# Attention by whole pairs of heads: 128-query tiles, plain float32 scores, single-bank ring, before two expert layers

## The chip, the cores and the metric

The kernel runs on one core of a Trainium2 chip. Five engines work from their own in-order queues: TensorE (PE, matrix products into PSUM), VectorE (DVE), ScalarE (ACT), GpSimd (POOL) and SyncE (SP, which here only issues transfers); they meet at semaphores. The metric is device microseconds of one execution, as a median of several.

## What is computed

```
# q, k, v: 2 batches x 12 heads x 448 positions x 64, float32
scores = q @ k.T / 8                    # causal: keys after the query are masked with -1e9
scores = scores - max(scores)
attn   = exp(scores);  attn = attn / (sum(attn) + 1e-9)
x      = attn @ v                       # to 896 tokens x 768
h      = x @ w_in;  g = max(h, 0) + alpha * min(h, 0);   x = g @ w_out      # 768 -> 2048 -> 768
h      = x @ w2_in; g = 0 if h <= -1, h if h >= 1, else (h + 1)**2 / 4;     out = g @ w2_out
```

The weights arrive as 64-bit floats.

## The kernel before

The 24 heads are taken as 12 pairs. A pair's q and k lie transposed in one tile (`qk_raw`): head 0 on partitions 0 to 63, head 1 on 64 to 127, so that the two heads of a score product occupy different halves of the rows of the PE array. The 448 queries of a head are four tiles of 112; tile i needs the first 112 (i + 1) keys. The loop at L451 walks over 48 tiles of 12 pairs. In step t it issues the scores of tile t, the exponentials and the normalisation of tile t - 1, the transposes of tile t - 3, the products with v of older tiles (first key chunk 7 steps behind, second 8, third and fourth 9), and the evacuation of a pair 10 steps behind. All of it is a hand-written order (`manual_schedule`): each engine executes its share in the order of the code.

For a tile with i > 0 the scores are three products of split operands (`qk_spl`: a rounded float32r part and the rest; L337 makes them, ACT the rounded part, POOL the rest); tile 0 uses the raw float32 values (L351). DVE reads the scores from PSUM, adds the mask and finds the row maximum in one operation (L363), ACT takes the exponential and its row sum (L373), DVE adds 1e-9 and inverts (L380, L381), POOL multiplies (L384), PE transposes 112 x 112 blocks (L394), ACT and DVE copy the result to `pt` (L400 to L405), and PE multiplies by v into `o_ps` (L413), both heads side by side in different column halves. The evacuation splits the result into x, a rounded part on ACT (L208) and the rest on DVE (L211).

On PE the groups of one pair come in this order: transposes of tile 2 (6), products with v of chunks 2 and 3 (224 and 112 columns of both heads), scores of tile 2 of the next pair (336 columns), transposes of tile 3 (8), scores of tile 3 (448), transposes of tile 0 (2), products with v of chunk 0 (448), scores of tile 0 (L351, 112), transposes of tile 1 (4), products with v of chunk 1 (336), scores of tile 1 (256). One plain float32 product is two instructions in the trace.

The 8 PSUM banks are three single ones for scores (`s_ps`), two tiles of two banks for transposes (`t_ps`) and one for `o_ps`. In the layers `new_banks` (L233) hands the same tiles out in turn, the two-bank tiles as two halves.

The weights come in chunks of 768 x 128 (first layer) through a ring of two raw buffers. A chunk is turned into a split pair by `magnitude` (L108, ACT), clamp (L124), low bits (L130), high bits (L136), last bits (L142, with a rounding copy on ACT, L145) and rest (L148), all on DVE but the two named. `prime` makes three chunks ready during the attention: from step 20 on it yields one operation in two of four steps. `early_tiles` issues products of the first layer for the x tiles that are ready, while the last pairs finish: 5 x 6 matmuls of the first output tile and 5 x 3 of the second. Then `run_layer` walks the four layers; its matmuls (L255) are 2304, with 448 columns each.

SP issues all loads in code order: per pair one transfer for q and k and one for v.

Of the kernel before, what the change touches and what calls it, by code (L numbers as in the profile page):

```python
# [22 lines left out]
def attention_moe_moe_kernel(ctx: ExitStack, tc: tile.TileContext, qk, v, w1, w2, w3, w4, alpha, out):  # L23
# [13 lines left out]
    W = [CP * (i + 1) for i in range(NQ)]  # L37
    OFF = [sum(W[:i]) for i in range(NQ)]
    TRI = sum(W)
# [6 lines left out]
    NSQ = 1  # L46
    NWARM = 9
# [10 lines left out]
    ident = const.tile([CP, CP], F32, tag="ident", name="ident")  # L58
    mask = const.tile([CP, S], F32, tag="mask", name="mask")
# [3 lines left out]
    def warm_up():  # L63

        z = const.tile([128, 512], F32R, tag="zero", name="zero")
        nc.vector.memset(f32(z), 0.0)
        for _ in range(NWARM):
            ps = ps_o.tile([128, 512], F32, tag="o", name="warm_ps")
            nc.tensor.matmul(ps, lhsT=z[:, :128], rhs=z, start=True, stop=True)  # L69

    def constants():
        nc.vector.memset(half, 0.5)
        make_identity(nc, ident)
        nc.gpsimd.memset(mask, 0.0)
        nc.gpsimd.affine_select(
            out=mask[:, S - CP:], in_=mask[:, S - CP:], compare_op=ALU.is_ge, fill=MASK,
            base=0, pattern=[[-1, CP]], channel_multiplier=1,
        )
# [154 lines left out]
    def new_banks():  # L233


        def one(pool, tag):
            return pool.tile([128, 512], F32, tag=tag, name="ps")

        while True:
            for singles in (((ps_s, "s"), (ps_s, "s")), ((ps_s, "s"), (ps_o, "o"))):  # L240
                for pool, tag in singles:
                    yield one(pool, tag)
                both = ps_t.tile([128, 1024], F32, tag="t", name="ps")
                yield both[:, :512]
                yield both[:, 512:]

    def new_tile():
        return next(banks)
# [58 lines left out]
    class Attention:  # L307
# [3 lines left out]

        PARTS = ((0, 0), (0, 1), (1, 0))

        def __init__(self, ap, ps_s, ps_t, ps_o):
            self.ap, self.ps_s, self.ps_t, self.ps_o = ap, ps_s, ps_t, ps_o
            self.raw, self.vraw, self.spl, self.pexp, self.st, self.pt, self.o = {}, {}, {}, {}, {}, {}, {}

        def load(self, p):
            t = self.raw[p] = self.ap.tile([2 * D, 2, S], F32, tag="qk_raw", name="qk_raw", bufs=3)
# [5 lines left out]
            t = self.vraw[p] = self.ap.tile([CP, NQ, 2, D], F32, tag="v_raw", name="v_raw", bufs=5)  # L328
            nc.sync.dma_start(out=t, in_=v[p])

        def split_qk(self, p, a, high=nc.scalar.copy, low=nc.gpsimd):
            t = self.raw[p]
            if a == 0:
                self.spl[p] = self.ap.tile([2 * D, 2, 2, S], F32R, tag="qk_spl", name="qk_spl", bufs=2)
            s = self.spl[p]
            n0 = NSQ * CP if a == 0 else 0
            high(s[:, a, 0, n0:], t[:, a, n0:])  # L337
            low.tensor_sub(s[:, a, 1, n0:], t[:, a, n0:], f32(s[:, a, 0, n0:]))

        def scores(self, p, i):  # L340
            if i == 0:
                self.pexp[p] = self.ap.tile([CP, 2, TRI], F32, tag="pexp", name="pexp", bufs=3)
                self.st[p] = self.ap.tile([CP, NQ, 3, 2], F32, tag="stat", name="stat", bufs=4)
            s, t = self.spl[p], self.raw[p]
            w = W[i]
            n = max(w, 256)
            ps = [self.ps_s.tile([128, 512], F32, tag="s", name="s_ps")[:CP] for _ in range(2)]
            if i < NSQ:
                for j in range(2):
                    r = slice(j * D, (j + 1) * D)  # L350
                    nc.tensor.matmul(  # L351
                        ps[j][:, :w], lhsT=t[r, 0, i * CP:(i + 1) * CP], rhs=t[r, 1, :w], start=True, stop=True
                    )
            for x, (a, b) in enumerate(self.PARTS if i >= NSQ else ()):
                for j in range(2):
                    r = slice(j * D, (j + 1) * D)
                    nc.tensor.matmul(  # L357
                        ps[j][:, :n], lhsT=s[r, 0, a, i * CP:(i + 1) * CP], rhs=s[r, 1, b, :n],
                        start=x == 0, stop=x == 2,
                    )  # L360

            for j in range(2):
                nc.vector.tensor_tensor_reduce(  # L363
                    out=self.pexp[p][:, j, OFF[i]:OFF[i] + w], in0=ps[j][:, :w], in1=mask[:, S - w:],
                    scale=-SCALE, scalar=3.0e38, op0=ALU.add, op1=ALU.min,
                    accum_out=self.st[p][:, i, 0, j:j + 1],
                )

        def expo(self, p, i):
            st = self.st[p]  # L370
            for j in range(2):
                e = self.pexp[p][:, j, OFF[i]:OFF[i] + W[i]]
                nc.scalar.activation(  # L373
                    out=e, in_=e, func=AF.Exp, bias=st[:, i, 0, j:j + 1], scale=-1.0,
                    accum_out=st[:, i, 1, j:j + 1],
                )

        def norm(self, p, i):
            st = self.st[p][:, i]
            nc.vector.tensor_scalar_add(st[:, 1], st[:, 1], 1e-9)  # L380
            nc.vector.reciprocal(st[:, 2], st[:, 1])  # L381
            for j in range(2):
                e = self.pexp[p][:, j, OFF[i]:OFF[i] + W[i]]
                nc.gpsimd.tensor_scalar(  # L384
                    out=e, in0=e, scalar1=st[:, 2, j:j + 1], scalar2=1.0, op0=ALU.mult, op1=ALU.mult
                )

        def transp(self, p, i):
            ps = self.ps_t.tile([128, 1024], F32, tag="t", name="t_ps")[:CP]
            ps = ps.rearrange("p (j n) -> p j n", j=2)[:, :, :S].rearrange("p j (c q) -> p j c q", q=CP)  # L390
            for j in range(2):
                for c in range(i + 1):
                    o = OFF[i] + c * CP
                    nc.tensor.transpose(ps[:, j, c, :], self.pexp[p][:, j, o:o + CP], ident)  # L394
            if i == 0:
                self.pt[p] = self.ap.tile([CP, 2, NQ, S], F32, tag="pt", name="pt", bufs=2)
            d = self.pt[p][:, :, :i + 1, i * CP:(i + 1) * CP]

            if i == 0:
                nc.scalar.copy(d, ps[:, :, :i + 1, :])  # L400
            elif i == 1:
                nc.vector.tensor_copy(d, ps[:, :, :i + 1, :])  # L402
            else:
                nc.scalar.copy(d[:, 0], ps[:, 0, :i + 1, :])
                nc.vector.tensor_copy(d[:, 1], ps[:, 1, :i + 1, :])  # L405

        def attnv(self, p, chunks):
            if 0 in chunks:
                self.o[p] = self.ps_o.tile([2 * D, 512], F32, tag="o", name="o_ps")
            ps, pt, vraw = self.o[p], self.pt[p], self.vraw[p]  # L410
            for c in chunks:
                for j in range(2):
                    nc.tensor.matmul(  # L413
                        ps[j * D:(j + 1) * D, c * CP:S], lhsT=vraw[:, c, j, :], rhs=pt[:, j, c, c * CP:S],
# [3 lines left out]
        def evac(self, p):  # L418
            b, m = divmod(p, NP // NB)
            interleave(evac_x(self.o.pop(p), m, b), [])  # L420

    with tc.manual_schedule():
        wts = Weights()
        ps_s, ps_t, ps_o = (
            ctx.enter_context(tc.tile_pool(name=f"ps_{n}", bufs=b, space=PSUM))
            for n, b in (("s", 3), ("t", 2), ("o", 1))
        )
        banks = new_banks()
        with ExitStack() as pa:
            ap = pa.enter_context(tc.tile_pool(name="attn", bufs=2))  # L430
            at = Attention(ap, ps_s, ps_t, ps_o)
            at.load(0)
            warm_up()
            nc.sync.dma_start(out=alpha_sb, in_=alpha)
            at.load(1)
            constants()
# [5 lines left out]
            NT = NP * NQ  # L442

            LE, LT = 1, 3
            LV = {7: (0,), 8: (1,), 9: (2, 3)}
            LX = 10
            PRIME = 20

            for t in range(NT + LX - 2):  # L451
                p, r = divmod(t, NQ)
                if t < NT:
                    at.scores(p, r)
                if t >= LX and (t - LX) % NQ == 0:
                    at.evac((t - LX) // NQ)
                if 0 <= t - LE < NT:
                    at.expo(*divmod(t - LE, NQ))
                    at.norm(*divmod(t - LE, NQ))
                if 0 <= t - LT < NT:  # L460
                    at.transp(*divmod(t - LT, NQ))
# [74 lines left out]
```

## Time and profile before

| | before |
|---|---|
| median of 3 runs | 586.44 us (584.26, 586.44, 595.68) |
| span of the profiled execution | 591.8 us |
| PE busy | 583.1 us (99%), 3009 matmuls |
| DVE busy | 442.3 us (75%) |
| ACT busy | 255.6 us (43%) |
| POOL busy | 161.6 us (27%) |
| matmuls of the layers (L255) | 240.2 + 238.6 us, 369 and 368 ns each, 2304 |
| granted TensorE clock, mean | 0.999 |

The shares of busy time are means over an attention part of some 120 us and four layers behind it. A busy PE is not PE at its peak, since matmuls are pipelined and an instruction's row also covers time in which it waits in the pipe; the distance from one start to the next tells more.

### The profile page before, as it was taken

How to read it: one execution, taken by the hardware profiler on the slowest of the kernel's cores; microseconds unless marked ns; L12 is line 12 of the kernel's file. 1: busy time of each engine (PE TensorE's matmuls, PEld its weight loads, DVE VectorE, ACT ScalarE, POOL GpSimd, SP SyncE). 2: the span in 40 equal slices, each digit the busy share in tenths (PEclk: the TensorE clock that was granted, in tenths of full speed). 3: DMA queues.
4: the chain of work that ended last, by engine and by line, in shares of the span. 5: the costliest groups of instructions: out<-in, count | busy, mean ns of one | idle time of the engine just before them, and what ended most of it. 6: DMA issues, size and time to landing. Idle time of an engine off the chain costs nothing.

```text
span 591.8 us, 8421 instructions
## 1 busy us (share of the span) xinstructions
PE 583.1 (99%) x3009; PEld 491.8 (83%) x3009; DVE 442.3 (75%) x894; ACT 255.6 (43%) x543; POOL 161.6 (27%) x190
## 2 busy tenths in 40 slices
PE   8999999999999999999999999999999999999997
PEld 3655555789999999999999999999999999999995
DVE  4899998488898898766657668888888867555740
ACT  3889888223333333333223325555555422222220
POOL 3777787223333343000000002333334300000000
PEclk9999999999999999999999999999999999999999
DMA  6533301113333222343324333333322244444420
GB/s 187 201 95 88 131 24 55 54 54 107 108 112 108 109 94 76 107 138 87 99 105 129 120 107 117 108 103 107 107 104 82 67 133 137 136 116 133 138 66 31
DMA packets 18569, 61.88 MB, mean 105 GB/s; under 512 B 2208, under 2 KB 5536, under 8 KB 18528
## 3 DMA queue, kind: packets, MB, share of 16 engines
q1 hardware_dynamic: 16656, 59.75, 32.3%
q10 hardware_dynamic: 1872, 1.61, 0.8%
q8 instruction: 23, 0.38, 0.2%
q14 instruction: 18, 0.15, 0.1%
HBM read 58.60 MB, written 2.75 MB: 104 GB/s over the span
## 4 chain that ended last, share of the span: by engine, by line
PE 95%; DVE 3%; ACT 1%; issue 0%; ACTq 0%; DVEq 0%
PE ps L255 81%; PE o_ps L413 5%; PE t_ps L394 4%; PE s_ps L357 4%; PE warm_ps L69 1%; DVE pexp L363 1%; PE s_ps L351 1%; DVE stat L380 0%; DVE pt L405 0%; DVE w_f L142 0%; DVE x L211 0%; ACT w_split L145 0%; ACT pexp L373 0%; DVE stat L381 0%; DVE pt L402 0%
## 5 line engine op out<-in xcount | busy, mean ns | idle before, releaser
L255 PE MATMUL ps<-x,w_split 128*128 128x448 f32 x1152 | 240.2, 369 | 0.2 <-DVE x L211 0.2
L255 PE MATMUL ps<-g,w_split 128*128 128x448 f32 x1152 | 238.6, 368 | 0.9 <-DVE o_sb L221 0.9
L255 PEld LDWEIGHTS ps<-x,w_split 128*128 128x128 f32 x1152 | 215.7, 188 | 24.4 <-issue 1.7
L255 PEld LDWEIGHTS ps<-g,w_split 128*128 128x128 f32 x1152 | 216.2, 188 | 23.0 <-DVE o_sb L221 1.3
L172 POOL TENSOR_TENSOR g<-act_g,g 128x448 fp32r<-128x448 f32 x64 | 85.6, 1337 | 281.4 <-ACT g L171 281.3
L145 ACT CAST w_split<-w_f 128x512 fp32r<-128x512 f32 (+1 forms) x80 | 56.6, 707 | 130.9 <-DVE w_f L142 90.9
L148 DVE TENSOR_TENSOR w_split<-w_f,w_split 128x512 fp32r<-128x512 f32 (+1 forms) x80 | 66.0, 825 | 53.6 <-ACT w_split L145 53.3
L171 ACT CAST g<-act_g 128x448 fp32r<-128x448 f32 x64 | 36.1, 564 | 79.2 <-DVE act_g L184 69.2
L136 DVE SCALAR_TENSOR_TENSOR w_f<-w_raw,w_f 128x512 uint32<-128x512 uint32 (+1 forms) x80 | 63.4, 793 | 1.4
L142 DVE SCALAR_TENSOR_TENSOR w_f<-w_raw,w_f 128x512 uint32<-128x512 uint32 (+1 forms) x80 | 63.4, 793 | 1.4
L124 DVE TENSOR_SCALAR w_f<-w_f 128x512 f32<-128x512 f32 (+1 forms) x80 | 58.1, 727 | 8.1 <-ACT w_f L108 7.9
L108 ACT ACTIVATE w_f<-w_raw 128x512 f32<-128x512 f32 (+1 forms) x80 | 61.3, 766 | 0.1
L384 POOL TENSOR_SCALAR pexp<-pexp,stat 112x112 f32<-112x112 f32 (+3 forms) x96 | 52.9, 564 | 24.4 <-DVE stat L381 19.3
L373 ACT ACTIVATE pexp<-pexp,stat 112x112 f32<-112x112 f32 (+3 forms) x96 | 49.9, 523 | 4.4 <-DVE stat L363 3.9
L363 DVE CUSTOM_DVE_ANT_0 pexp<-s_ps,mask 112x112 f32<-112x112 f32 (+3 forms) x96 | 39.1, 445 | 7.8 <-PE s_ps L351 4.6
L130 DVE TENSOR_SCALAR w_f<-w_f 128x512 uint32<-128x512 uint32 (+1 forms) x80 | 38.0, 475 | 1.4
L196 ACT ACTIVATE act_t<-act_t,half 128x448 f32<-128x448 f32 x32 | 21.5, 671 | 39.5 <-DVE act_t L195 39.5
L413 PE MATMUL o_ps<-pt,v_raw 112*64 112x448 f32 (+3 forms) x192 | 36.8, 418 | 0.0
L394 PE MATMUL t_ps<-ident,pexp 112*112 112x112 f32 x240 | 34.5, 276 | 0.0
L394 PEld LDWEIGHTS t_ps<-ident,pexp 112*112 112x112 f32 x240 | 23.9, 138 | 10.5 <-issue 5.3
L357 PE MATMUL s_ps<-qk_spl 64*112 64x256 f32 (+2 forms) x216 | 30.3, 374 | 2.2 <-DVE stat L363 2.2
L221 DVE COPY o_sb<-ps 128x224 f32<-128x224 f32 x12 | 4.7, 392 | 32.3 <-ACT o_sb L221 32.3
(38 smaller groups left out, 286.0 us busy)
## 6 DMA issues: line engine op xcount, KB each, us to landing
w_raw<-w SPq DMA_DIRECT2D x32, 768.0 KB, 4.3
w_raw<-w SPq DMA_DIRECT2D x48, 512.0 KB, 3.6
qk_raw<-qk SPq DMA_DIRECT2D x11, 448.0 KB, 3.7
v_raw<-v SPq DMA_DIRECT2D x12, 224.0 KB, 3.2
out<-o_sb SPq DMA_DIRECT2D x12, 112.0 KB, 1.7
out<-o_sb ACTq DMA_DIRECT2D x12, 112.0 KB, 1.7
qk_raw<-qk ACTq DMA_DIRECT2D x1, 224.0 KB, 3.5
qk_raw<-qk SPq DMA_DIRECT2D x1, 224.0 KB, 3.3
```

The lines of the kernel that those rows point to most:

```text
L108: nc.scalar.activation(out=f32(w), in_=f32(hi), func=AF.Abs)
L124: nc.vector.tensor_scalar(out=f32(w), in0=f32(w), scalar1=HI_MIN, scalar2=HI_MAX, op0=ALU.max, op1=ALU.min)
L136: nc.vector.scalar_tensor_tensor(out=w, in0=hi, scalar=0xC0000000, in1=w, op0=ALU.bitwise_and, op1=ALU.bitwise_or)
L142: nc.vector.scalar_tensor_tensor(out=w, in0=lo, scalar=29, in1=w, op0=ALU.logical_shift_right, op1=ALU.bitwise_or)
L145: nc.scalar.copy(s[:, 0, :n], f32(w))
L148: nc.vector.tensor_sub(s[:, 1, :n], f32(w), f32(s[:, 0, :n]))
L172: nc.gpsimd.tensor_sub(t[:, 1, :], g, f32(t[:, 0, :]))
L255: nc.tensor.matmul(ps[b][:, :S], lhsT=ws[:, part, k * 128:(k + 1) * 128], rhs=src[b, kk][:, xp, :], start=first and part == 0 and xp == 0, ...
L357: nc.tensor.matmul(ps[j][:, :n], lhsT=s[r, 0, a, i * CP:(i + 1) * CP], rhs=s[r, 1, b, :n], start=x == 0, stop=x == 2,)
L384: nc.gpsimd.tensor_scalar(out=e, in0=e, scalar1=st[:, 2, j:j + 1], scalar2=1.0, op0=ALU.mult, op1=ALU.mult)
L394: nc.tensor.transpose(ps[:, j, c, :], self.pexp[p][:, j, o:o + CP], ident)
L413: nc.tensor.matmul(ps[j * D:(j + 1) * D, c * CP:S], lhsT=vraw[:, c, j, :], rhs=pt[:, j, c, c * CP:S], start=c == 0, stop=c == NQ - 1,)
```

## The change

The unit of the loop becomes a whole pair. Queries are cut into three tiles of 128 (i = 0, 1, 2) and a last one of 64, whose two heads share one tile (i = 3): head 0 on partitions 0 to 63, head 1 on 64 to 127 of one bank. All scores use the raw float32 values; the split of q and k is gone. Step n issues, for pair n, all scores; for pair n - 2, the products with v and the evacuation; for pair n - 1, the transposes and copies. PSUM becomes a ring of seven single banks for scores, transposes, warming matmuls and layer tiles, and one bank for `o_ps`. Rows of v are repacked into 128-row chunks by seven transfers per pair. Two operations of `prime` follow at the end of each step from n = 2 on. `early_tiles` works on one output tile instead of two. The warming matmuls are four instead of nine, and q and k of pair 1 are issued ahead of v of pair 0.

```diff
-    NSQ = 1
-    NWARM = 9
+    NV = 4
+    NWARM = 4
...
-            ps = ps_o.tile([128, 512], F32, tag="o", name="warm_ps")
+            ps = bank()
             nc.tensor.matmul(ps, lhsT=z[:, :128], rhs=z, start=True, stop=True)
...
+    def bank():
+        return ps_s.tile([128, 512], F32, tag="s", name="ps")
+
+    new_tile = bank
...
+        def load_v(self, p):
+            t = self.v[p % NV]
+            for c in range(NQ):
+                n = CP - 16 * c
+                nc.sync.dma_start(out=t[:n, c], in_=v[p, 16 * c:, c])
+                if c + 1 < NQ:
+                    nc.sync.dma_start(out=t[n:, c], in_=v[p, :128 - n, c + 1])
...
+        def scores(self, p, i):
             t = self.raw[p]
...
+            if i == 3:
...
+                ps = bank()
                 for j in range(2):
                     r = slice(j * D, (j + 1) * D)
+                    nc.tensor.matmul(ps[r, :S], lhsT=t[r, 0, 384:S], rhs=t[r, 1], start=True, stop=True)
+                return [ps]
+            ps = [bank(), bank()]
+            w = 128 * (i + 1)
             for j in range(2):
+                r = slice(j * D, (j + 1) * D)
+                nc.tensor.matmul(
+                    ps[j][:, :w], lhsT=t[r, 0, w - 128:w], rhs=t[r, 1, :w], start=True, stop=True
+                )
+            return ps
...
+        def inverse(self, p, half):
+            st = self.st[p][:, :, :3] if half == 0 else self.st[p][:, :, 3:]
             nc.vector.tensor_scalar_add(st[:, 1], st[:, 1], 1e-9)
             nc.vector.reciprocal(st[:, 2], st[:, 1])
...
-            ctx.enter_context(tc.tile_pool(name=f"ps_{n}", bufs=b, space=PSUM))
-            for n, b in (("s", 3), ("t", 2), ("o", 1))
+            ctx.enter_context(tc.tile_pool(name=f"ps_{n}", bufs=b, space=PSUM)) for n, b in (("s", 7), ("o", 1))
...
-            at.split_qk(0, 0, nc.vector.tensor_copy, nc.vector)
-            at.split_qk(0, 1, nc.vector.tensor_copy, nc.vector)
             early = {}
-            fill = early_tiles(((0, 1), (0,)))
+            fill = early_tiles(((0, 1),))
...
+            for n in range(NP + 2):
+                cp, ev = {}, []
+                new, old, out_p = n < NP, 0 <= n - 1 < NP, 0 <= n - 2 < NP
+                ps = {i: at.scores(n, i) for i in (3, 2, 1, 0)} if new else {}
+                if n == NP + 1:
+                    step(fill, 8)
+                if out_p:
+                    at.attnv(n - 2)
+                    ev = at.evac(n - 2)
+
+                if new:
+                    at.low(n, 3, ps[3])
+                    at.expo(n, 3)
+                if old:
+                    at.inverse(n - 1, 1)
+                if old:
+                    for i in (3, 2, 1, 0):
+                        cp[i] = at.transp(n - 1, i)
+                if n >= NP:
+                    step(fill, 4 if n == NP else 30)
+                if new:
+                    for i in (2, 1, 0):
+                        at.low(n, i, ps[i])
+                    at.expo(n, 2)
+                    at.expo(n, 1)
+                    at.inverse(n, 0)
+                if ev:
+                    ev[0]()
+                if new:
+                    at.expo(n, 0)
+                if old:
+                    nc.vector.tensor_copy(*cp[3][0])
+                    nc.vector.tensor_copy(*cp[2][0])
+                    nc.scalar.copy(*cp[2][1])
+                    nc.scalar.copy(*cp[1][0])
+                if ev:
+                    ev[1]()
+                if old:
+                    nc.vector.tensor_copy(*cp[0][0])
+                if n + 3 < NP:
+                    at.load_qk(n + 3)
+                if n + 1 < NP:
+                    at.load_v(n + 1)
+                if n == 1:
                     wts.load()
                     wts.load()
+                if n >= 2:
+                    step(prime, 2)
```

On PE, in the middle of the attention, these rows follow each other before the change (`t_ps` are transposes, `s_ps` scores, `o_ps` products with v; the waits name engines):

```order
L413 MATMUL o_ps<-pt,v_raw 64x448 [waits DMAHW5_49,DVE_49,Activation_49]
L413 MATMUL o_ps<-pt,v_raw 64x448 [waits DVE_49]
L351 MATMUL s_ps<-qk_raw 112x112 [waits DMAHW0_49]
L351 MATMUL s_ps<-qk_raw 112x112 [waits DVE_49]
L394 MATMUL t_ps<-ident,pexp 112x112 [waits PE_49,Pool_49]
L394 MATMUL t_ps<-ident,pexp 112x112
L394 MATMUL t_ps<-ident,pexp 112x112 [waits Pool_49]
L394 MATMUL t_ps<-ident,pexp 112x112
L413 MATMUL o_ps<-pt,v_raw 64x336 x2
L357 MATMUL s_ps<-qk_spl 112x256 [waits DVE_49] x2
L357 MATMUL s_ps<-qk_spl 112x256 x4
```

And after it, where a step begins (`ps` is any bank of the ring; L333 and L339 are scores, L416 products with v):

```order
L333 MATMUL ps<-qk_raw 64x448 [waits DMAHW4_49,DVE_49]
L333 MATMUL ps<-qk_raw 64x448
L339 MATMUL ps<-qk_raw 128x384 [waits DVE_49] x2
L339 MATMUL ps<-qk_raw 128x256 [waits Activation_49]
L339 MATMUL ps<-qk_raw 128x256 [waits DVE_49]
L339 MATMUL ps<-qk_raw 128x128 [waits Activation_49]
L339 MATMUL ps<-qk_raw 128x128 [waits DVE_49]
L416 MATMUL o_ps<-pt,v_82 64x448 [waits DMAHW6_49,DMAHW5_49]
L416 MATMUL o_ps<-pt,v_82 64x448
L416 MATMUL o_ps<-pt,v_82 64x320 [waits DMAHW7_49,DMAHW0_49]
L416 MATMUL o_ps<-pt,v_82 64x320
```

The groups of several tiles that alternated now stand in one block for each kind of work, all scores of a pair first, each a single plain product for a head; the last scores wait for ACT and DVE.

On DVE, in the middle of the attention, before (L363 reduces scores, L380 and L381 invert, L405 copies a transpose, L211 makes the rest of x):

```order
L211 TENSOR_TENSOR x_0_367<-o_ps,x_0_367 128x448 [waits Activation_49]
L380 TENSOR_SCALAR stat<-stat 112x2 [waits Activation_49]
L381 RECIPROCAL stat<-stat 112x2 [waits DVE_49]
L405 COPY pt<-t_ps 112x4x112 [waits Activation_49]
L363 ISA pexp,stat<-s_ps,mask 112x448 [waits PE_49]
L363 ISA stat 112x1
L363 ISA pexp,stat<-s_ps,mask 112x448 [waits PE_49]
L363 ISA stat 112x1
L380 TENSOR_SCALAR stat<-stat 112x2 [waits Activation_49]
L381 RECIPROCAL stat<-stat 112x2 [waits DVE_49]
```

And after, around the end of step 2, where the first weight operation stands (L126 is the clamp, L350 the score reduction, L479 to L486 copies of transposes, L366 and L367 the inversion):

```order
L367 RECIPROCAL stat<-stat 128x3 [waits DVE_49]
L479 COPY pt<-ps 128x4x2x64 [waits PE_49]
L480 COPY pt<-ps 128x3x128 [waits PE_49]
L213 TENSOR_TENSOR x_0_283<-o_ps,x_0_283 128x448 [waits Activation_49]
L486 COPY pt<-ps 128x2x128 [waits PE_49]
L126 TENSOR_SCALAR w_f_347<-w_f_347 128x768 [waits Activation_49]
L350 ISA pexp,stat<-ps,mask_66 128x448 [waits PE_49,Pool_49]
L350 ISA stat 128x1
L366 TENSOR_SCALAR stat<-stat 128x4
L367 RECIPROCAL stat<-stat 128x4 [waits DVE_49]
L350 ISA pexp,stat<-ps,mask 128x384 [waits PE_49]
```

All copies of a pair stand together at the end of a step, and the weight operations behind them, ahead of the first reduction of the next step; the clamp waits for ACT.

## Rows read from the trace of the kernel before

**Rows 1.** Windows, two stretches: time in us, busy us and instructions of each engine, clock, DMA.

```profile
0.00:20.00 20.00, 17.35 (x60) 9.28 (x61) 9.78 (x43) 9.23 (x28) 8.73 (x21) 1.00 0.62 186
40.00:60.00 20.00, 20.00 (x160) 12.27 (x158) 18.79 (x72) 18.05 (x58) 16.40 (x27) 1.00 0.35 105
```

**Rows 2.** Chain of waits, 0 to 60 us: start, us, what held the end.

```profile
9.08 0.70 PE s_ps L351 x4
...
40.79 0.72 PE t_ps L394 x6
41.50 0.72 PE o_ps L413 x8
42.23 0.65 PE s_ps L357 x6
42.87 0.91 PE t_ps L394 x8
43.78 0.79 PE s_ps L357 x6
44.58 0.33 PE t_ps L394 x2
44.91 1.37 PE o_ps L413 x4
46.28 0.38 PE s_ps L351 x4
46.66 0.53 PE t_ps L394 x4
47.18 0.72 PE o_ps L413 x4
47.90 0.53 PE s_ps L357 x6
```

**Rows 3.** Chain of waits, 60 to 140 us.

```profile
69.47 1.66 PE o_ps L413 x4
...
94.45 1.69 PE o_ps L413 x4
...
114.17 0.90 PE o_ps L413 x4
...
120.66 19.48 PE ps L255 x93
```

**Rows 4.** Timeline of DVE in one pair: start, us, operation, idle before.

```profile
45.17 0.61 DVE L363 CUSTOM_DVE_ANT_0 pexp<-s_ps,mask 112x448 f32<-112x448 f32 x1
...
45.71 0.62 DVE L363 CUSTOM_DVE_ANT_0 pexp<-s_ps,mask 112x448 f32<-112x448 f32 x1
...
46.80 0.27 DVE L363 CUSTOM_DVE_ANT_0 pexp<-s_ps,mask 112x112 f32<-112x112 f32 x1 [0.18 <-PE s_ps L351]
...
47.00 0.27 DVE L363 CUSTOM_DVE_ANT_0 pexp<-s_ps,mask 112x112 f32<-112x112 f32 x1
```

**Rows 5.** Groups by line and form, 0 to 130 us: count, busy us, mean ns.

```profile
L108 ACT ACTIVATE w_f<-w_raw 128x768 f32<-128x768 f32 x5 | 4.6, 922 | 0.0
...
L142 DVE SCALAR_TENSOR_TENSOR w_f<-w_raw,w_f 128x768 uint32<-128x768 uint32 x4 | 3.8, 950 | 0.0
...
L145 ACT CAST w_split<-w_f 128x768 fp32r<-128x768 f32 x4 | 3.3, 833 | 5.7 <-DVE w_f L142 5.7
L124 DVE TENSOR_SCALAR w_f<-w_f 128x768 f32<-128x768 f32 x5 | 3.3, 658 | 0.3 <-ACT w_f L108 0.3
L130 DVE TENSOR_SCALAR w_f<-w_f 128x768 uint32<-128x768 uint32 x5 | 2.7, 550 | 0.0
```

**Rows 6.** Timeline, start: a transfer issued on SP, the first cast on DVE.

```profile
3.53 0.43 SPq L329 DMA_DIRECT2D v_raw<-v  x1
...
4.01 0.34 DVE L337 CAST qk_spl<-qk_raw 128x336 fp32r<-128x336 f32 x1 [2.61 <-DMA qk_raw<-qk]
```

**Rows 7.** Timeline, end of the kernel, PE.

```profile
585.59 2.70 PE L255 MATMUL ps<-g,w_split 128*128 128x448 f32 x12 [0.90 <-DVE o_sb L221]
```

More of the change, by code (lines that the diff above doesn't have):

```diff
@@ L73, in constants @@
         make_identity(nc, ident)
[L74 to L78, printed above, removed]
+        for m, rows, n in ((mask, slice(0, 128), 128), (mask3, slice(0, 64), 64), (mask3, slice(64, 128), 64)):
+            nc.gpsimd.memset(m[rows], 0.0)
+            d = m[rows, m.shape[1] - n:]
+            nc.gpsimd.affine_select(
+                out=d, in_=d, compare_op=ALU.is_ge, fill=MASK, base=0, pattern=[[-1, n]], channel_multiplier=1
+            )
     class Weights:
@@ L231, in interleave @@
                     ops.pop(0)()
[L233 to L248, printed above, removed]
+    def bank():
+        return ps_s.tile([128, 512], F32, tag="s", name="ps")
+    new_tile = bank
     def products(ps, ws, src, k, kk, first, last):
@@ L307, in attention_moe_moe_kernel, with __init__, load_qk @@
     class Attention:
[L315 to L322, printed above, removed]
+        def __init__(self, ap):
+            self.ap = ap
+            self.raw, self.pexp, self.st, self.pt, self.o = {}, {}, {}, {}, {}
+            self.v = [ap.tile([128, NQ, 2, D], F32, tag=f"v{i}", name=f"v{i}", bufs=1) for i in range(NV)]
+            for t in self.v:
+                nc.gpsimd.memset(t[64:, NQ - 1], 0.0)
+        def load_qk(self, p):
+            t = self.raw[p] = self.ap.tile([2 * D, 2, S], F32, tag="qk_raw", name="qk_raw", bufs=4)
             if p == 0:
@@ L367, in scores @@
                 )
         def expo(self, p, i):
-            st = self.st[p]
-            for j in range(2):
-                e = self.pexp[p][:, j, OFF[i]:OFF[i] + W[i]]
+            for j in range(1 if i == 3 else 2):
+                o, w, n = self.place(i, j)
+                e = self.pexp[p][:, o:o + w]
                 nc.scalar.activation(
-                    out=e, in_=e, func=AF.Exp, bias=st[:, i, 0, j:j + 1], scale=-1.0,
-                    accum_out=st[:, i, 1, j:j + 1],
-                )
@@ L407, in attnv @@
[L407 to L411, printed above, removed]
+            for i in (3, 2) if half == 0 else (1, 0):
+                for j in range(1 if i == 3 else 2):
+                    o, w, n = self.place(i, j)
+                    e = self.pexp[p][:, o:o + w]
+                    nc.gpsimd.tensor_scalar(
+                        out=e, in0=e, scalar1=self.st[p][:, 2, n:n + 1], scalar2=1.0, op0=ALU.mult, op1=ALU.mult
+                    )
@@ new lines, in step @@
+            def step(gen, n):
+                for _ in range(n):
+                    next(gen, None)
+            for n in range(NP + 2):
[41 more added lines that the diff above has]
+                if n == 1:
@@ L473, in attention_moe_moe_kernel @@
                     wts.load()
                     wts.load()
-                if t >= PRIME and r in (0, 3) or t >= NT:
-                    next(prime, None)
-                if t >= NT:
-                    for _ in range(2):
-                        next(fill, None)
+                if n >= 2:
+                    step(prime, 2)
             for _ in fill:
```

154 lines of the change are left out of this document (61 added, 93 removed).

## The prediction

> **What bounds the kernel now.** I read the busy time by stretch first. In a steady stretch of the attention every engine is nearly full [rows 1]: PE 20.0 of 20 us, DVE 18.8, ACT 18.1, POOL 16.4. So no share of busy time names the bound, and I went to the chain of waits, which tiles time without overlap. In it the reader is to see that one pair of heads costs eleven PE pieces that add up to 7.64 us (40.79 to 48.43), with no other engine between them [rows 2]. Only one piece holds a wait: the first product with v takes 1.37 us there and 0.90 where nothing holds it [rows 2, 3]. So PE has 7.17 us of work per pair and 0.47 us of waiting. In the later pairs, where the first weight chunks are split on DVE beside the attention, three pairs take 94.45 - 69.47 = 24.98 us, 8.33 each: there DVE and ACT join the chain. The layers behind 120.66 us run at 19.48 / 93 = 0.2095 us per matmul [rows 3], and the change leaves them alone but for their last gap. So the case is decided between 0 and 120.66 us.
>
> **Prices for PE.** Transposes: 8 take 0.91 and 2 take 0.33 [rows 2], so 0.097 each and 0.14 for the start. At 128 columns instead of 112 one is 0.111, so the 16 of a step cost 1.77 + 0.14 = 1.91 (20 in four groups cost 2.49). Products with v: 336 columns of both heads take 0.72, 448 take 0.90 [rows 2, 3]: 1.61 ns per column and 0.18. The new 448 + 320 + 192 + 64 = 1024 columns, in one group, cost 1.65 + 0.18 = 1.83 (2.34 unhindered before). Scores: the trace has plain float32 ones only for the first query tile: 0.38 for both heads at 112 columns [rows 2]. If the two heads, on different halves of the array's rows, ran one after the other, 0.18 + 2 x 0.18 = 0.54 would stand there; side by side, 0.36. I take side by side. The split products bear it out: three couples take 0.53 at 256 columns and 0.79 at 448, so 0.45 ns per column and couple, where a single matmul of the layers takes 0.2095 / 448 = 0.47. 448 + 384 + 256 + 128 = 1216 columns at 1.61 are 1.96, and two layouts (64 and 128 output rows) add 0.36: 2.32, as much as the old 0.38 + 0.53 + 0.65 + 0.79 = 2.35. Sum for a step: 6.06 us, against 7.17 + 0.47.
>
> The 448-wide score is new in kind: two row halves write one bank. Bounds: 0.72 as taken, and 1.44 if the heads take turns.
>
> **Prices for DVE.** Reductions follow each other by 0.54 us at 448 columns (45.17 to 45.71) and 0.20 at 112 (46.80 to 47.00) [rows 4]: 1.01 ns per column and 0.09. The seven of a step (448, twice 384, 256 and 128) cost 2.61. Two inversions per step instead of four: between 45.71 + 0.54 and 46.80 lie 0.55 us, of which 0.18 is idle, so 0.37 each, 0.74. Copies out of the transposes (512, 384, 256 columns) at the same slope: 1.42. The low half of x, 448 wide: 0.54. Sum 5.31. ACT loses the rounding of q and k and POOL its two subtractions; neither is on the path then.
>
> **Weight chunks.** Three chunks are split in steps 2 to 11, two operations a step. One chunk is 0.66 + 0.55 + 3 x 0.95 = 4.06 us of DVE (the high, last and rest operations are alike; one row stands), and 0.92 + 0.83 on ACT [rows 5]. The two per step fall in cycles of three steps: magnitude and clamp, low and high bits, last bits and rest. Here the change adds waits, since the two stand back to back. The clamp follows a magnitude that ACT starts only after its two copies. Its wait is between 0 (ACT early) and one copy and the magnitude, 0.5 + 0.92; I take 1.3, near the upper end, because both engines reach their last copy at about the same time. The rest waits for ACT's rounding, 0.83, with handover 0.9. Behind both stands the next step's first reduction, and behind that the next pair's exponentials. So the steps are 5.31 + 0.66 + 1.3 = 7.27, 5.31 + 0.55 + 0.95 = 6.81 and 5.31 + 1.90 + 0.9 = 8.11: DVE is late, not PE (6.06). Three cycles are 66.6, the eleventh step is PE's 6.06, and the first steps take up 2 x 0.75 of DVE's slack: 71.1 us for ten steps.
>
> **Start and end.** Scores now start at 9.08, behind nine warming matmuls, though q and k are in at 4.01, where DVE begins to cast them [rows 2, 6]. Four warming matmuls without the split let them start at 4.3 (at the old spacing they would end by 4.9). At the start the same four matmuls of the first query tile take 0.70, and 0.38 later [rows 2]: I read it as TensorE at the lower of its two levels (1.2 against 2.4 GHz), although the granted clock shows 1.00 in both stretches [rows 1]. So the first scores cost 4.6; the second scores and the first transposes between 4.2 and 8.5, I take 5.3, since PE then works without the gaps it had. Step 2 begins at 14.2. Ten steps: 85.3. Then 2 for the last copies of pair 10, 1.83 + 1.91, thirty filling matmuls 6.29, 1.83, and 1.2 for x (two passes of 448): 100.4. With 1 us for handovers, 101.4, where before 120.66 stands. Fifteen filling matmuls fewer lie ahead of that point (30 in the code, not 45): 3.14 come back. At the very end PE waits 0.90 us for the copy of the other half of a two-bank tile [rows 7]; with single banks nothing holds it: -0.9. **Sum: 591.8 - 19.3 + 3.1 - 0.9 = 574.7**, 17.1 us less. The profiled span is 5.4 above the median of the runs, so the same 17.1 goes off 586.4: **569**.
>
> At nothing I cost: seven transfers for v in place of one. With q and k that is eight issues of 0.43 on SP [rows 6], 3.4 us a step under 7.1, for tiles used two steps later; without that cover 3 us per step would be at stake. Masks and zeroed v rows are a few operations on POOL before the first reduction, which comes after 5 us. Seven banks: a step takes twelve, so the last scores wait for the previous step's last copies, which are behind only by the half of a microsecond that the earlier scores cover.
>
> **Rivals.**
> (a) The wait at the split of the weights costs more, or PE stays at the lower level to 20 us as before: +3.2 at the start, or up to +6.6 with those waits doubled: 572 to 579. For it: DVE's margin is small [rows 1]. Chance 0.12.
> (b) The heads take turns on the plain scores altogether: PE 6.06 + 1.96 = 8.02 a step, above all of DVE's sums but one. Ten steps are 80.2, the start 3.9 later: 17.1 - 13 leaves 4, so 582. The 0.38 speaks against it. Chance 0.11.
> (c) Only the one-bank scores take turns: 6.78 a step, still under DVE's, so between 2 and 12 x 0.72 = 8.6 us: 571 to 578. In the kernel before the two heads' scores lie in separate banks, so no row tells. Chance 0.08. The Trainium skill speaks for this one (TensorEngine Tiling (Array Packing), Gotcha 1: PSUM Pressure): different row tiles cannot use one PSUM bank at the same time. No run here shows it yet.
> (d) Slower than before: TensorE falls to the lower level during the attention, because PE now waits a microsecond per step for DVE and has its transposes in one block. A step is then 12.1 instead of 7.1; from six of the ten steps on (6 x 5 > 17.1 + 11.7) the kernel is slower by over 2%, with all ten 619. Against it: the granted clock is 1.00 in the steady stretch, where 2.5 of 7.64 us are transposes and the later pairs, longer and with waits, keep their rate. Chance 0.05. The Trainium skill would favour it (TensorE: Matmul & The Clock Gate, Part 4: PE-mode transpose): transposes do not count as activity for the clock. The row above disagrees as far as it goes.
> (e) The waits at the weights hide fully: ten steps nearer 6.06 than 7.1, up to -10: 559 to 562. Chance 0.06.
>
> **Numbers.** The forecast itself, 562 to 575, has 0.58. About 2% is what a measurement of this kernel can tell from no change: below 574.7 is faster, above 598 slower. Faster: 0.58 + 0.06, half of (c) and a third of (a), 0.72. Slower: (d), 0.05. The rest, 0.23, is within 2%. A range of 562 to 581 reaches into (b) and leaves (d), most of (b) and half of (e) out.
>
> **What would show it.** Right: first scores near 4.3 us, PE groups of 2.3, 1.8 and 1.9 us per step, the 128-column scores of both heads in about 0.4, a step of 6.1 without and 7 to 8 with weight operations, with DVE idle before the clamp and the rest for ACT, the layers starting near 101. Wrong: scores of a step above 4 us (b), the 448-wide one at 1.4 (c), matmuls of doubled duration in the steady steps (d), or a PE that waits in every step for a bank, which my walk of the ring leaves out.

## The result: 3.3% faster, as forecast, and the profile after

The changed kernel takes 566.5 us as a median of four executions, against 585.7 for the kernel before: a ratio of 0.967 (95% interval 0.9645 to 0.9691), some 19 us less. The forecast was 569 in a range of 562 to 581. The executions of all these kernels fall into two groups about 1.6% apart, in which a matmul of the layers takes 0.203 or 0.207 us; ratios compare the faster group, and the two traces of before and after are both of the slower one, so they may be laid side by side: 591.8 us of span became 573.1, 18.7 less, where the sum had 17.1.

The stretches that answer to [rows 1], from the windows view (us, busy us of PE, PE's loads, DVE, ACT and POOL, then granted clock, DMA share, GB/s):

```profile
0.00:20.00 20.00, 17.32 (x100) 10.23 (x100) 12.28 (x59) 13.76 (x47) 11.52 (x33) 1.00 0.65 196
40.00:60.00 20.00, 19.54 (x136) 11.71 (x133) 17.50 (x62) 15.49 (x50) 9.46 (x20) 1.00 0.57 175
```

POOL fell from 16.4 to 9.5 us of 20 and ACT from 18.1 to 15.5, and DVE is still nearly full (17.5). In the chain of waits, one step without a hindrance and the head of one with it answer to the pair of [rows 2] (start, us, what held the end):

```profile
20.20 0.90 PE ps L333 x4
21.10 1.50 PE ps L339 x12
22.60 1.88 PE o_ps L416 x16
24.48 0.58 PE ps L388 x4
25.07 0.66 PE ps L396 x6
25.72 0.66 PE ps L406 x6
...
46.84 0.90 PE ps L333 x4
47.74 2.18 PE ps L339 x11
49.92 1.88 PE o_ps L416 x16
...
85.12 3.11 PE o_ps L416 x16
...
99.97 15.14 PE ps L245 x72
```

The first six rows are all of PE's work for one pair: scores 0.90 + 1.50, products with v 1.88, transposes 0.58 + 0.66 + 0.66, in sum 6.18 us where the old order had 7.64. Against the old groups the transposes save 0.59 us (1.90 for 2.49), the products with v 0.46 (1.88 for 2.34) and the wait ahead of them 0.47, and the scores cost 0.05 more. In the seventh and eighth row the scores take 0.68 longer, because the banks of the ring wait for DVE and ACT. The layers start at 99.97 instead of 120.66 [rows 3].

What DVE does in between answers to [rows 4, 5], from its timeline (the bracket is the idle time ahead and what ended it):

```profile
41.36 0.41 DVE L486 COPY pt<-ps 128x256 f32<-128x256 f32 x1
43.17 0.56 DVE L126 TENSOR_SCALAR w_f<-w_f 128x768 f32<-128x768 f32 x1 [1.40 <-ACT w_f L110]
43.65 0.62 DVE L350 CUSTOM_DVE_ANT_0 pexp<-ps,mask 128x448 f32<-128x448 f32 x1
...
48.72 0.55 DVE L132 TENSOR_SCALAR w_f<-w_f 128x768 uint32<-128x768 uint32 x1
...
57.10 0.96 DVE L150 TENSOR_TENSOR w_split<-w_f,w_split 128x768 fp32r<-128x768 f32 x1 [0.90 <-ACT w_split L147]
```

Here the two waits that the change adds are to be read: the clamp stands 1.40 us for its magnitude, the rest 0.90 us for the rounding. From the first reduction (43.65) to the next weight operation (48.72) DVE works through one pair in 5.07 us without a gap. At the start, the timeline of PE answers to [rows 6]:

```profile
1.45 2.08 PE L70 MATMUL ps<-zero 128*128 128x512 f32 x4 [1.45 <-DVE half L73]
4.03 1.76 PE L333 MATMUL ps<-qk_raw 64*64 64x448 f32 x4 [0.50 <-DMA qk_raw<-qk]
...
7.95 0.97 PE L333 MATMUL ps<-qk_raw 64*64 64x448 f32 x4
```

The first scores start when k lands, and the second pair's already run at the upper level: 0.97 for what took 1.76 four microseconds earlier. And at the end the group of the last layer's matmuls in the page shows no idle time ahead of it, where [rows 7] had 0.90:

```profile
L245 PE MATMUL ps<-g,w_split 128*128 128x448 f32 x1152 | 238.4, 368 | 0.0
```

### The profile page after: what moved, and what is told of

The parts are those of the page before. It is cut to its first block, busy times and chain, and to the rows that moved or that the text cites. A ratio compares the mean times of both kernels' runs of the same rounds, so it can differ in the third digit from the quotient of the medians.

```text
span 573.1 us, 8115 instructions
## 1 busy us (share of the span) xinstructions
PE 562.7 (98%) x2884; PEld 484.9 (85%) x2884; DVE 421.8 (74%) x818; ACT 237.4 (41%) x485; POOL 129.4 (23%) x164
## 4 chain that ended last, share of the span: by engine, by line
PE 93%; DVE 3%; ACT 3%; DMA 1%; issue 1%; ACTq 0%
PE ps L245 83%; PE o_ps L416 3%; PE ps L339 2%; ACT pexp L359 2%; PE ps L333 1%; DVE pexp L350 1%; PE ps L396 1%; PE ps L406 1%; PE ps L388 1%; DMA qk_raw<-qk 1%; DVE x L213 0%; ACT x L210 0%; DVE pt L479 0%; ACT pt L482 0%; DVE stat L367 0%
## 5 line engine op out<-in xcount | busy, mean ns | idle before, releaser
L126 DVE TENSOR_SCALAR w_f<-w_f 128x512 f32<-128x512 f32 (+1 forms) x80 | 58.1, 727 | 12.2 <-ACT w_f L110 11.8
L359 ACT ACTIVATE pexp<-pexp,stat 128x384 f32<-128x384 f32 (+3 forms) x84 | 43.8, 522 | 17.7 <-DVE stat L350 17.7
L372 POOL TENSOR_SCALAR pexp<-pexp,stat 128x384 f32<-128x384 f32 (+3 forms) x84 | 40.6, 501 | 41.8 <-DVE stat L367 39.6
L350 DVE CUSTOM_DVE_ANT_0 pexp<-ps,mask 128x384 f32<-128x384 f32 (+3 forms) x84 | 32.8, 444 | 5.4 <-PE ps L333 4.6
L339 PEld LDWEIGHTS ps<-qk_raw 64*128 64x128 f32 x144 | 14.9, 191 | 15.3 <-DVE pt L479 3.5
L416 PE MATMUL o_ps<-pt,v 128*64 128x448 f32 (+3 forms) x192 | 24.6, 401 | 2.6 <-ACT pt L482 2.6
L416 PEld LDWEIGHTS o_ps<-pt,v 128*64 128x64 f32 x192 | 13.2, 141 | 14.0 <-issue 6.6
L181 DVE TENSOR_SCALAR act_t<-ps,alpha_sb 128x448 f32<-128x448 f32 x32 | 21.8, 680 | 3.5 <-PE ps L245 2.5
```

The source lines that it names most:

```text
L126: nc.vector.tensor_scalar(out=f32(w), in0=f32(w), scalar1=HI_MIN, scalar2=HI_MAX, op0=ALU.max, op1=ALU.min)
L350: nc.vector.tensor_tensor_reduce(out=self.pexp[p][:, o:o + w], in0=b[:, :w], in1=mask3 if i == 3 else mask[:, 384 - w:], scale=-SCALE, sca ...
L359: nc.scalar.activation(out=e, in_=e, func=AF.Exp, bias=self.st[p][:, 0, n:n + 1], scale=-1.0, accum_out=self.st[p][:, 1, n:n + 1],)
L372: nc.gpsimd.tensor_scalar(out=e, in0=e, scalar1=self.st[p][:, 2, n:n + 1], scalar2=1.0, op0=ALU.mult, op1=ALU.mult)
L416: nc.tensor.matmul(ps[j * D:(j + 1) * D, c * 128:S], lhsT=t[:, c, j, :], rhs=pt[:, j, c * 448:c * 320 + S], start=c == 0, stop=c == NQ - 1,)
```

## Experiments

Two theories had to be kept apart all along: that the gain comes from PE's path (an earlier start, fewer hindrances, cheaper groups), and that it comes from the work taken off ACT and POOL. Lowest times of one execution are given for comparison: 584.3 to 584.9 for the kernel before in all series, 563.6 to 564.0 for the changed one. In the first series of runs (the pairing, the filling products, the old warming, the plain scores) one of the four times behind each ratio to the kernel before is 593.6, beside 584.9 to 585.6; those ratios are too low by some 0.003, and their intervals are wide.

**The weight operations paired one later.** This parts the clamp from its magnitude and the rest from its rounding by a whole step.

```diff
-                    step(prime, 2)
+                    step(prime, 1 if n == 2 else 2)
```

> The weight operations of the attention are paired one later: step 2 issues one, every later step two, so that a clamp stands a step behind its magnitude and a rest a step behind its rounding. Theory (the two waits of DVE on ACT, 1.4 and 0.9 us per chunk, set the length of the steps with weight work): they vanish, steps 4 to 11 fall from about 7.0 towards the sum of DVE's work, 6.3 to 6.9, and the kernel gains 3 to 6 us on the changed one (561 to 564). Rival (DVE only waits there because PE is behind anyway): less than 1 us, 566.

Lowest 557.3, median 558.1, a ratio of 0.951 to the kernel before (0.942 to 0.959). That is 6.5 us under the changed kernel: the theory, and a little beyond its range. Starts of a step on PE, and the two operations on DVE, from the timelines:

```profile
38.76 0.97 PE L333 MATMUL ps<-qk_raw 64*64 64x448 f32 x4
...
45.26 0.97 PE L333 MATMUL ps<-qk_raw 64*64 64x448 f32 x4
...
51.43 0.97 PE L333 MATMUL ps<-qk_raw 64*64 64x448 f32 x4
...
57.60 0.97 PE L333 MATMUL ps<-qk_raw 64*64 64x448 f32 x4
```

```profile
40.29 0.95 DVE L150 TENSOR_TENSOR w_split<-w_f,w_split 128x768 fp32r<-128x768 f32 x1
...
46.23 0.55 DVE L126 TENSOR_SCALAR w_f<-w_f 128x768 f32<-128x768 f32 x1
```

Neither operation has a bracket any more, and three steps take 57.60 - 38.76 = 18.84 us instead of 21.4 (39.73 to 61.09 in the timeline of the changed kernel). Two of the three are back at PE's own 6.17.

**Filling products ahead of the last products with v.** In step 12 no scores are left, and PE stands before the products with v of pair 10 until ACT has copied that pair's last transposes (the bracket is the idle time, in the trace shown above):

```profile
85.12 3.11 PE L416 MATMUL o_ps<-pt,v 128*64 128x448 f32 x16 [2.60 <-ACT pt L482]
```

```diff
-                if n == NP + 1:
-                    step(fill, 8)
+                if n >= NP:
+                    step(fill, 4 if n == NP else 8)
...
-                if n >= NP:
-                    step(fill, 4 if n == NP else 30)
+                if n > NP:
+                    step(fill, 30)
```

> In the step after the last scores, the four products of the first layer that fill PE are issued ahead of the products with v instead of behind the transposes. Theory (PE stands idle for 2.6 us there, waiting for the copies of pair 10, and its granted clock falls to 0.50 behind that gap): both go, the first product with v in that step takes 1.9 us instead of 3.1, and the kernel gains 3 to 4.5 us (562 to 563.5). Rival (the copies come later by the same amount, or the fall of the clock has nothing to do with the gap): 0 to 2.6 us.

Lowest 561.5, median 562.0, ratio 0.957 (0.946 to 0.967). The chain of waits shows the filling matmuls in the gap, and the products with v at full pace behind them:

```profile
82.54 4.87 PE ps L245 x24
87.41 1.88 PE o_ps L416 x16
...
95.69 29.45 PE ps L245 x144
```

The layers start 4.3 us earlier than in the trace of the changed kernel, yet the lowest times differ by 2.1 to 2.5 only. The windows view of the changed kernel, in the same trace, gives the reason:

```profile
85.00:86.00 1.00, 0.88 (x4) 0.34 (x6) 0.00 (x0) 0.90 (x2) 1.00 (x3) 0.88 0.00 0
86.00:88.00 2.00, 2.00 (x14) 1.18 (x10) 0.00 (x0) 0.00 (x0) 0.57 (x2) 0.50 0.00 0
```

In this trace the granted clock falls to 0.50, the lower level, just behind the idle 2.60 us, and the products with v take 3.11 us instead of 1.88.

**The changed kernel again**, on the chip of the later runs:

> The changed kernel itself, on the same chip as the other three, to compare them with: 564 to 567 and a ratio near 0.967.

Lowest 563.6, ratio 0.964 (0.962 to 0.966). The windows view of its trace, 84 to 90 us:

```profile
84.00:90.00 6.00, 5.33 (x41) 4.39 (x42) 2.31 (x7) 2.94 (x6) 1.71 (x5) 1.00 0.01 3
```

Here the clock stays at 1.00 behind the same idle 2.60 us, and the layers start at 97.77, 13.10 us after the products with v (84.67); the first trace has 14.85 between the two (85.12 to 99.97). So the gap itself is worth about 2 us (97.77 against 95.69), and the fall another 1.75, in some executions only.

The mean granted clock, recorded for every execution, tells which. Of the thirteen traces the five with a mean of 0.997 show the fall behind the gap, and no other does. The changed kernel took 563.6, 564.0 and 564.6 us at a mean of 0.999 or 1.000, and 566.5 and 566.6 at 0.996 or 0.997; its three executions near 575 all have 0.997. None of the twelve executions of versions that fill the gap (this one, and the two at the end) is below 0.999. So filling the gap also takes the fall away: the gain is 2.1 to 2.5 us against the lowest times, and 4.5 against the executions with the fall, the upper end of what was expected.

**The old warming.** Nine matmuls through one bank, in the changed kernel.

```diff
-    NWARM = 4
+    NWARM = 9
...
-            ps = bank()
+            ps = ps_o.tile([128, 512], F32, tag="o", name="warm_ps")
```

> The changed kernel with the warming of the kernel before: nine matmuls that follow each other through the one bank of the products with v. Theory (5 us of the gain came from scores that start when q and k are in): first scores at 9.1 instead of 4.0, the kernel 4.5 to 6 us slower than the changed one (571 to 572.5). Rival (the start is hidden, since DVE and ACT bound the first steps): under 2 us. A third possibility: the warming buys an earlier rise to the upper level, which would give 1 to 2 us of it back.

Lowest 568.9, 4.9 to 5.3 above the changed kernel. The chain of waits has the first scores at 9.07 and the layers at 104.58 (99.97 in the changed kernel):

```profile
9.07 1.69 PE ps L333 x4
...
104.58 20.52 PE ps L245 x98
```

The first scores take 1.69 there, so TensorE is at the lower level behind nine warming matmuls as it is behind four, and the second pair's scores, 3.8 us later (12.79), are at the upper level as they were there: the third possibility falls.

**No warming at all**, in the changed kernel (`NWARM = 0`):

> The changed kernel with no warming matmuls. Theory (the dense scores raise TensorE to its upper level by themselves): first scores still at 4.0 and at the lower level, the rise at most 3.5 us later than with four, the time within -1 and +3 us of the changed kernel. Rival (the four matmuls ahead of the scores buy the early rise): the first 12 us or more at the lower level, +3 to +6 us.

Lowest 563.9, ratio 0.964 (0.962 to 0.966), the same as the changed kernel. PE's timeline, with the second pair's scores already at the upper level:

```profile
4.20 1.76 PE L333 MATMUL ps<-qk_raw 64*64 64x448 f32 x4 [4.20 <-DMA qk_raw<-qk]
...
8.46 0.97 PE L333 MATMUL ps<-qk_raw 64*64 64x448 f32 x4
```

So the four matmuls buy nothing that can be measured; the dense scores raise the clock.

**The kernel before without warming** (`NWARM = 0` there):

> The kernel before without its nine warming matmuls, everything else as it was: the part of the start that the change could have had by itself. Theory (the warming chain, not the split of q and k, held the first scores until 9.1): first scores near 4.5, the scores that need the split near 6, and 3 to 5 us less than the kernel before (580 to 582). Rival (without them TensorE stays at the lower level so much longer that nothing is won): within 1 us.

Lowest 581.9, ratio 0.995 (0.993 to 0.998): 2.4 to 2.9 us, just short of what was expected. First scores at 4.19, but the layers start only 2.76 us earlier (117.90). PE's timeline tells where the rest went:

```profile
4.19 0.72 PE L351 MATMUL s_ps<-qk_raw 64*112 64x112 f32 x4 [4.19 <-DMA qk_raw<-qk]
...
17.97 1.45 PE L357 MATMUL s_ps<-qk_spl 64*112 64x448 f32 x6
```

In the old order the scores of 448 columns still take 1.45 us at 17.97, and 0.79 later [rows 2]: the lower level lasts to 19 us, with warming matmuls or without. In the changed kernel it ended by 8. The same chain is worth 5 us in the new order and 2.8 in the old one. Of the 2.1 us that are missing there, some 0.9 are gone before the first transposes (10.46 against 14.39, with the first scores at 4.19 against 9.08), while the scores wait for DVE and the split operands; 1.1 go behind that at the lower level, where the eight transposes at 16.30 take 1.74 instead of 1.20 and the scores behind them 1.45 instead of 0.86.

**Plain scores in the old order.** The kernel before, with float32 scores for all query tiles and no split of q and k:

```diff
-    NSQ = 1
+    NSQ = NQ
...
-            at.split_qk(0, 0, nc.vector.tensor_copy, nc.vector)
-            at.split_qk(0, 1, nc.vector.tensor_copy, nc.vector)
...
-                    if r == 0:
-                        at.split_qk(p + 1, 0)
-                    elif r == 1:
-                        at.split_qk(p + 1, 1)
-                    elif r == 3 and p + 2 < NP:
+                    if r == 3 and p + 2 < NP:
```

> The kernel before with plain float32 scores for all four query tiles and no split of q and k, everything else as it was: that one part of the change alone. Theory (plain scores cost PE what the split ones did, and the gain lies in the order and the tiles): PE's groups of scores take 0.38, 0.55, 0.72 and 0.90 instead of 0.38, 0.53, 0.65 and 0.79, a pair stays between 7.3 and 7.9 us, and the time is 582 to 588. Rival (the split on ACT and POOL was the real load, 0.8 us of ACT and 2.0 of POOL per pair): pairs of 6.9 us or less, 575 to 578.

Lowest 581.9, ratio 0.993 (0.982 to 1.004): not told apart from the kernel before. The chain of waits over one pair (31.20 to 38.91 in the same manner):

```profile
38.91 1.15 PE o_ps L413 x4
40.06 0.38 PE s_ps L351 x4
...
41.68 0.57 PE s_ps L351 x4
...
43.69 0.75 PE s_ps L351 x4
...
45.35 0.94 PE s_ps L351 x4
...
46.62 1.15 PE o_ps L413 x4
```

Scores of 0.38, 0.57, 0.75 and 0.94, a pair of 7.71 us, and no piece of another engine in the chain. The scores cost PE 0.29 us more than the split ones (2.64 against 2.35), and the product with v that waits took 1.15 instead of 1.37. So taking 0.8 us of ACT and 2.0 us of POOL off every pair bought at most 0.2 of the 1.46 us, because PE sets the pair. The rest of the gain is in the order, the tiles and the start. No run has the order without the tiles, so these two are not parted.

**Heads in turn.** The changed kernel, with the three tiles of head 0 ahead of those of head 1:

```diff
-            for j in range(2):
-                r = slice(j * D, (j + 1) * D)
...
+            for j in range(2):
+                for i in (2, 1, 0):
+                    r = slice(j * D, (j + 1) * D)
```

> The changed kernel with the scores of the three 128-query tiles issued head by head (all three of head 0, then all three of head 1) instead of tile by tile. Neighbouring matmuls then use the same half of the array's rows. Theory (two heads side by side are what keeps plain scores at 2.4 us a step): the six products take 2.6 to 2.9 us instead of 1.5, the steps grow by about 1.2 where PE sets them and less where DVE does, and the time is 572 to 580. Rival (PE streams one product after the other anyway): no change, 564 to 566.

573.7 (two executions, 573.7 and 582.9): 10 us above the lowest time of the changed kernel, 7 above its executions with the same mean clock (566.5 at 0.996). The chain of waits over one step:

```profile
27.46 0.90 PE ps L333 x4
28.36 2.25 PE ps L343 x10
30.60 1.88 PE o_ps L419 x16
...
34.38 0.90 PE ps L333 x4
```

The six products take 2.25 instead of 1.50, and the step 6.92 instead of 6.18. That two heads run side by side is shown by this. The size was expected at 2.6 or more; that the last product of head 0 and the first of head 1 still overlap may be the difference, and is not shown. The time fell into the expected range for another reason. In this trace the layers start at 107.98, 8.0 us later than in the first trace of the changed kernel, and 7.3 of that are there when the fourth pair's scores start (27.39 against 20.13); the eight steps behind add 1.4 only, since most of them took about 7 us in the changed kernel too, set by DVE. The start is where it is lost, because TensorE stays at the lower level through three pairs:

```profile
19.68 1.75 PE L333 MATMUL ps<-qk_raw 64*64 64x448 f32 x4
```

**v in one transfer.** The host lays v out in chunks of 128 rows, padded with zeros:

```diff
-            for c in range(NQ):
-                n = CP - 16 * c
-                nc.sync.dma_start(out=t[:n, c], in_=v[p, 16 * c:, c])
-                if c + 1 < NQ:
-                    nc.sync.dma_start(out=t[n:, c], in_=v[p, :128 - n, c + 1])
+            nc.sync.dma_start(out=t, in_=v[p])
```

> The changed kernel with v laid out on the host in chunks of 128 rows, padded with zeros, and one transfer per pair instead of seven. Theory (SP's issues and the small packets lie beside other work): the time stays within 1.5 us of the changed kernel, and the wait of ACT for the first weight chunk shortens at most. Rival (eight transfers per step hold SP, and the weight chunks come late): 2 us or more faster.

Lowest 565.4, ratio 0.966 (0.965 to 0.968), against 0.964 for the changed kernel measured beside it: no gain, rather 1.8 us the other way. All four executions have a mean granted clock of 0.997, and the trace shows the fall at 85 us; the changed kernel's executions with the fall took 566.5 and 566.6, about 1 us more. So the seven transfers cost at most about 1 us. They are not quite hidden: in the second trace of the changed kernel ACT stands 0.65 us at 20.40 for the first weight chunk, which is issued behind the transfers of v, and by the chain of waits the step from 25.21 takes 6.59 us instead of 6.17 for that. In the first trace, which started 1.1 us later, and with one transfer there is no such wait.

**Both edits, and the end covered.** First the two edits together:

> Both edits together: weight operations paired one later, and the first layer's products issued ahead of the products with v in the step after the last scores. Theory (the waits at the weights and the idle 2.4 us behind the last scores are separate pieces of PE's path): the gains add, the layers start near 90 us instead of 100, and the time is 554 to 557. Rival (with the weight waits gone the copies of pair 10 come in time, so the fill has nothing to cover): as with the pairing alone, 557 to 560.

Lowest 555.6, ratio 0.950 (0.948 to 0.951); the layers start at 89.83. The gains add: 1.7 us below the pairing alone, and the layers start 2.4 earlier (92.26 there). Then a second output tile among the filling products, whose matmuls stand behind the last products with v:

```diff
-            fill = early_tiles(((0, 1),))
+            fill = early_tiles(((0, 1), (0,)))
...
-                    step(fill, 4 if n == NP else 8)
+                    step(fill, 4 if n == NP else 1)
```

> The version with both edits, and five products of the second output tile (first batch, 15 matmuls) issued behind the last products with v, to cover the evacuation of the last pair. Theory (PE stands there for 1.2 us): 1 us less than the version with both edits, 554.5 to 555. Rival (the 15 matmuls only move): no change.

Lowest 553.8, median 554.9, ratio 0.948 (0.947 to 0.950). The ratios of the two versions overlap, so the gain of about 1 us rests on the traces: in both the last scores start at 70.33, the layers start at 89.83 without the fifteen matmuls, and with them PE's timeline has no gap left between the last products with v and the layers:

```profile
86.49 1.95 PE L416 MATMUL o_ps<-pt,v 128*64 128x448 f32 x16
88.37 11.82 PE L245 MATMUL ps<-x,w_split 128*128 128x448 f32 x57
```

This version beats both kernels: 5.2% under the kernel before, where the change made 3.3 to 3.6%.

## Why the prediction was right, step by step

**The bound.** That PE's path, and not the full DVE, ACT and POOL, set the old pair was the step on which the rest stood. Plain scores in the old order show it: with the load of ACT and POOL gone a pair still took 7.71 us, all of it in PE's pieces.

**PE's prices** held within 4%: scores 2.40 (2.32 predicted), products with v 1.88 (1.83), transposes 1.90 (1.91), 6.18 in sum (6.06). Side by side was right, and heads in turn prices the contrary at 0.75 us a step. Rival (b) falls. So does (c): both heads' 448-wide scores write one bank in 0.90 us, the 0.72 and 0.18 of the sum, and not 1.62. The Trainium skill's rule that different row tiles cannot use one PSUM bank at the same time (TensorEngine Tiling (Array Packing), Gotcha 1: PSUM Pressure) does not show here as lost time; in this kernel the two row tiles also write different partitions of the bank, and the rule as the page puts it makes no such difference. The measurement decides.

**The waits at the weights** came as predicted, 1.40 and 0.90 us against 1.3 and 0.9, and their price is shown by the shifted pairing: the sum held 3 x 2.2 = 6.6 us for them, and 6.5 went with them. DVE's own sum was 0.24 too high (5.31; 5.07 measured). A cycle of three steps took 21.4 instead of 22.2, and ten steps 68.6 (13.81 to about 82.4) instead of 71.1. So the sum lay 2.5 us high there.

**Start and end.** Scores at 4.03 (4.3 predicted), step 2 at 13.81 (14.2). The reason given for the start, the chain of warming matmuls, holds in the new order, where the old warming costs 4.9 to 5.3 us; taken out of the old order it gives 2.8, so there the early scores alone are not enough. Step 12 was mis-sized: 2 us of waiting were in the sum, 2.6 came, and in the trace shown the fall of the clock another 1.75, which the sum did not have. In total the layers start at 99.97 in that trace and 97.77 in the other, against 101.4: the sum was 0.4 high at the start, 2.5 high in the ten steps and 1.5 low behind them. The last gap of 0.90 us went as predicted, and the fifteen matmuls came back: from the start of the layers to the end it is 471.1 before and 473.1 after, and 471.1 + 3.1 - 0.9 is 473.3. The span was thus missed by 1.6 us only (574.7 forecast, 573.1 measured). That it is so little is partly luck, since DVE's price and the end erred in opposite directions; the mechanism does not hang on it.

**The clock.** Rival (d) did not come: the granted clock is 1.00 in all full steps, in which 1.9 of 6.2 us are transposes, and the matmuls keep the durations of the upper level. The Trainium skill holds that transposes do not count as busy time in the same way (TensorE: Matmul & The Clock Gate, Part 4: PE-mode transpose); whether they do or not, at this share they cost nothing. A fall to the lower level did come, behind the one idle stretch of 2.6 us. Rival (a) did not come in the changed kernel's traces, whose lower level ended by 8 us; the heads in turn show that it can last past 20. Rival (e) did not come either, and the shifted pairing shows what it would have been worth.

**Priced at nothing**: the seven transfers (at most about 1 us, as shown above), the ring of seven banks. Of the ring, the scores that wait for copies (2.18 instead of 1.50) are the delay of DVE passed on: with the weight waits gone two steps of three are back at 6.17. A ring of another size was not tried.

## What to carry to other kernels

When every engine is nearly full, build the sum from the chain of waits, piece by piece: the engines that look as busy as the bound may be emptied without any gain. Background work that hops between two engines should put a whole step between its halves; back to back, each hop is a wait of the engine that everybody needs. Behind the last iteration of a pipeline, look at what stands idle for the drain, and put ready work of the next stage there rather than behind it.

## What was not expected of the hardware

Nine warming matmuls, each waiting for the one before, do not raise TensorE's clock: the scores behind them still take 1.69 us where they take 0.90 later. Behind the scores of the first pair in one block it rose in most traces: with no warming at all those at 4.2 us are at the lower level and those at 8.5 at the upper. In the old order of small groups with waits the lower level lasted to 19 or 20 us. But the block alone does not fix the moment. The version with both edits starts with the same code as the changed kernel, and its second pair's scores are still at the lower level:

```profile
8.55 1.76 PE L333 MATMUL ps<-qk_raw 64*64 64x448 f32 x4
```

With the heads in turn the third pair's are, at 19.68. What decides is left open.

The granted clock is not told by its column at the start, where it reads 1.00 while the same matmuls take twice as long; at 86 us it does show 0.50, and the transposes that follow the products with v take 1.05 us instead of 0.59.

Behind the same idle stretch of 2.4 to 2.6 us the clock fell in five traces (the changed kernel's first among them, 0.50) and not in two (its second, and the shifted pairing, 1.00). What decides between them is left open too; with the stretch filled it never fell.
